# Pooled attention and a top-1 expert layer on one core: partial sums of keys moved up, and the pooled keys of later batches turned by VectorE and a trip through DRAM

## The chip, the core and the metric

The kernel runs on one core of a Trainium2 chip. The metric is the time of one execution on the device in microseconds (us): 2063.51 us is the median of three runs of the kernel before (2062.11 to 2064.42). TensorE (PE in the profile) does matrix products, VectorE (DVE) and ScalarE (ACT) work element by element, GpSimd (POOL) does so too and issues scattered transfers, and SyncE's queue (SP) issues nearly all other DMA transfers.

## The reference, cut to what matters

```python
# q: 4 x 12288 x 128, kv: 4 x 384 x 32 x 128, w_sr: 128 x 128
kv_pool = kv.reshape(B, H // 4, 4, W // 4, 4, C).mean(axis=(2, 4))   # 768 keys for each batch
k = v = kv_pool.reshape(B, -1, C) @ w_sr
a = softmax(q @ k.T / sqrt(C))
x = (a @ v).reshape(B * N, C)                                        # 49152 tokens
# a layer of 8 experts (128 -> 1024 -> 128): each token goes to its best expert
expert = argmax(x @ w_gate); gate = softmax(x @ w_gate)[expert]
out = gate * (relu(x @ w1[expert]) @ w2[expert])
```

## The kernel before

The 49152 tokens are worked off in 96 tiles of 512. For each tile the kernel forms the scores against the batch's 768 keys, the softmax, the weighted values, the choice of expert, and the expert layer with the expert that most tokens of the tile (or of two neighbouring tiles) chose; the tokens left over are worked off at the end. All large products are three products of split numbers (`mm3`, lines 293 to 296): high times high, high times low, low times high. So one product shows as lines L294, L295 and L296.

Everything is written into one plan, `at(t, function)`, and the plan is emitted in order of `t`. A tile is 16 units of plan time. The table `AT` holds the offsets. The plan has no effect on the chip but the order of the instructions on each engine: each engine works its queue in order and waits where an operand is not there. SP's queue is in order too, so a transfer that waits holds up all transfers behind it.

Keys come in six blocks of 128 for each batch (`keys`, L301). A block's raw rows are 16 vectors for each key, 1 MB in four transfers (L317).

- First batch (`b` is 0): loaded at the very start, before anything else can run. Blocks 0 and 2 are summed by VectorE in eight reductions (L335) and turned by one TensorE transpose (L343). Blocks 1, 3, 4 and 5 are summed and turned by TensorE at once, with 16 products against the identity that accumulate (L325). The first q tile is loaded by four transfers (L289) between blocks 2 and 3.
- Later batches: one block every 48 units, which is three tiles, some twenty tiles ahead of use. VectorE sums it in eight reductions spread over the time (`pool` 22.7, step 3.5, so the last stands at 47.2), then `turn` (47.27) puts one 128x128 transpose on TensorE (L343), which writes to a PSUM bank.

After that the two ways are the same: `mean` copies the turned block from PSUM to SBUF on ScalarE with the factor 1/16 (L347), `project` multiplies it twice by `w_sr` on TensorE (L358, L359), and `high_kv` and `low_kv` split the results into `kh`, `vh` (ScalarE) and `kl`, `vl` (VectorE). The turn and the projection each take one PSUM bank from the pool that the expert layer's products use.

The first six tiles turn their probabilities by TensorE; all later ones turn 32x32 squares on VectorE (L473) and finish the turn by writing to DRAM (`pd<-pb`, L480) and reading back in another order (`pt<-pd`, L491 or L495). In the trace the names are those of the tiles: `pooled` is the sum of a block, `pooledT` its turned form, `pt`, `pth`, `pb` probabilities or, early, raw keys and weights, `hh` and `hlow` the expert's hidden values, `wt` its weights.

Of the kernel before, what the change touches and what calls it, by code (L numbers as in the profile page):

```python
# [30 lines left out]


AT = {
    "keys": -0.65, "load": 3.81, "loads": 2.45, "pool": 22.7, "pools": 3.5, "turn_k": 47.27, "turn_q": 2.25,
    "high_q": 4.43, "low_q": 6.71, "maxima": 0.94, "exps": 1.78, ("first_p", 0): 6.14, ("first_p", 1): 3.88,
    ("first_p", 2): 4.75, ("first_p", 3): 4.14, ("first_p", 4): 4.69, ("first_p", 5): 7.37, "first_high": 0.45,
    "first_low": 1.47, "first_values": 2.68, "turn_p": 2.71, ("send_p", 0): 9.0, ("send_p", 1): 16.32, ("fetch_p",
    0): 12.18, ("fetch_p", 1): 22.11, ("high_p", 0): 28.75, ("high_p", 1): 31.23, ("high_p", 2): 31.41, "low_p":
    2.88, ("values", 0): 32.61, ("values", 1): 37.47, ("values", 2): 38.87, ("values", 3): 38.06, ("values", 4):
    40.04, ("values", 5): 41.81, "copy_x": 0.6, "turn_x": 2.61, "logits": 0.46, "gate_exp": 5.86, "gate": 7.55,  # L40
    "ranks": 0.42, "home": 1.04, "places": 4.21, "put_x": 5.65, "high_x": -0.89, "low_x": 3.3, "begin": 83.05,
    "begin_raw": 55.73, "where": -11.29, "raw_cut": -0.42, "raw_cuts": 3.72, "single": 7.95, "spare": -0.19, "ends":
    64.6, "turn_m": -1.68, "high_m": 0.53, "low_m": 3.37, "first": 4.6, "high_h": 0.39, "low_h": 1.61, "second":
    4.8, "copy_y": 0.35, "pads": 3.85, "split": -7.13, "splits": 13.77, "split_cut": 4.58, "split_keep": 8.34,
    "turn_y": 1.84, "move_y": 0.65, "fetch_y": 6.15, "order_y": 13.25, "store_y": 14.0, "rows_y": 4.66, "small":
    -62.58, "square_x": -2.0, "keep_x": 6.88, ("fetch_w", 0): 38.97, ("fetch_w", 1): 47.76, "turn_q_first": -1.28,
    "high_q_first": 5.95, "low_q_first": 11.25, "maxima_first": 0.95, "exps_first": 1.78, "copy_x_first": 0.6,
    "turn_x_first": 2.61, "logits_first": 0.31, "gate_exp_first": 5.2, "gate_first": 9.09, "ranks_first": 0.72,
    "home_first": 0.92, "places_first": 5.56, "put_x_first": 6.88, "high_x_first": 2.66, "low_x_first": 4.03,
    "square_x_first": -2.28, "keep_x_first": 4.32, "turn_q_last": 2.09, "high_q_last": 0.49, "low_q_last": 4.66,  # L50
    "maxima_last": 0.8, "exps_last": 1.78, "turn_p_last": 2.64, ("last", "send_p", 0): 9.0, ("last", "send_p", 1):
    18.25, ("last", "fetch_p", 0): 14.25, ("last", "fetch_p", 1): 20.87, ("last", "high_p", 0): 28.51, ("last",
    "high_p", 1): 31.23, ("last", "high_p", 2): 31.41, "low_p_last": 2.75, ("last", "values", 0): 32.61, ("last",
    "values", 1): 39.93, ("last", "values", 2): 37.08, ("last", "values", 3): 39.31, ("last", "values", 4): 40.04,
    ("last", "values", 5): 41.81, "copy_x_last": 1.6, "turn_x_last": 2.61, "logits_last": 1.96, "gate_exp_last":
    5.86, "gate_last": 7.55, "ranks_last": 0.42, "home_last": 1.03, "places_last": 4.21, "put_x_last": 6.72,
    "high_x_last": -0.83, "low_x_last": 3.3, "square_x_last": -1.7, "keep_x_last": 6.86, ("late", 0): 0.0, ("late",
    1): 0.0, ("late", 2): 16.47, ("half", 0): 67.27, ("half", 1): 74.89, "read": 9.0, ("gather", 0): 18.15,
    ("gather", 1): 15.91, "gathers": 16.0, "count": 62.0, "ask": 74.77, "order_y_first": 11.43, "order_y_last":
    9.25, "store_y_first": 12.26, "store_y_last": 10.0, ("tile", 0): 0.0, ("tile", 1): 0.0, ("tile", 2): -0.02,  # L60
    ("tile", 3): 0.0, ("tile", 4): 0.0, ("tile", 5): 0.02, ("tile", 6): -0.15, ("tile", 7): 0.0, ("tile", 8): 0.0,
    ("moe", 0): 0.2, ("moe", 1): 0.27, ("moe", 2): 0.12, ("moe", 3): 0.69, ("moe", 4): 0.07, ("moe", 5): -0.44,
    ("moe", 6): -3.41, ("moe", 7): 0.0, "where_raw": -8.43, "weights_raw": -5.73, ("weights", 0): -10.38,
    ("weights", 1): -0.95,
}
# [19 lines left out]
def tile_pooled_attention_top1_moe(ctx: ExitStack, tc, q, kv, w_sr, w_gate, w1, w2, out):  # L85
# [215 lines left out]
    def keys(t, b, step):  # L301
        kvv = kv[b].rearrange("(hb i) (wb j) c -> hb wb i (j c)", i=POOL, j=POOL)
        own = {}

# [65 lines left out]
        def high_kv(kb):  # L370
            pr = own["pr", kb]
            src = ordered(pr[:, :P])
            nc.scalar.mul(out=columns(own["kh"], kb), in_=src, mul=scale)
            high(own["vh"][:, kb], pr[:, P : P + C])

        def low_kv(kb):
            pr = own["pr", kb]
            src = ordered(pr[:, :P])
            nc.vector.scalar_tensor_tensor(
                out=columns(own["kl"], kb), in0=src, scalar=scale, in1=columns(own["kh"], kb).bitcast(F32),  # L380
                op0=ALU.mult, op1=ALU.subtract,
            )
# [852 lines left out]
```

## Time and profile before

| what | value |
|---|---|
| median of three runs | 2063.51 us |
| the profiled execution | 2064.57 us, of which the trace's span is 2062.8 us |
| busy share of the span, TensorE / VectorE / GpSimd / ScalarE | 97% / 80% / 73% / 70% |
| chain of work that ended last: TensorE / VectorE / DMA | 81% / 7% / 4% |
| DMA | 484.79 MB, 235 GB/s on average |

Matrix products are pipelined, and their spans in the trace overlap: a 128x512 product shows as 0.39 us, but the next one starts 0.23 to 0.24 us later. So the busy share of TensorE says little; the distance between the starts of two products says what one costs.

### The profile page before, as it was taken

The numbers are of one execution on the slowest core, as the hardware profiler recorded it, in microseconds if no ns is written. First come the engines' busy times: TensorE is split into PE (matmuls) and PEld (weight loads), VectorE is DVE, ScalarE is ACT, GpSimd is POOL, SyncE is SP. The second block draws the span as 40 slices with busy tenths as digits, with TensorE's granted clock in tenths as the row PEclk, the third lists the DMA queues.
The fourth block names the chain that finished last, engine by engine and source line by source line (L and its number), as shares of the span: only waits on it lengthen the run. The fifth ranks groups of instructions, "written<-read, shape, count | busy, mean of one in ns | idle before, by whom it ended". The sixth has DMA issues, their size and how long they took to land.

```text
span 2062.8 us, 32814 instructions
## 1 busy us (share of the span) xinstructions
PE 1994.2 (97%) x9642; PEld 1658.0 (80%) x9642; DVE 1650.5 (80%) x3340; ACT 1442.2 (70%) x2775; POOL 1514.5 (73%) x1589
## 2 busy tenths in 40 slices
PE   6899899999999999999999999999999999999998
PEld 5677678888888888888888888888888888888877
DVE  4678788888888888888788888888877888788755
ACT  3676666777777777777777767677677777767654
POOL 2776677777777777677777777776778777778872
PEclk9999999999999999999999999999999999999999
DMA  9899999898789878877778978787778978777651
GB/s 233 264 270 263 253 229 237 231 237 222 219 260 298 246 229 243 231 244 220 230 228 278 290 225 239 227 256 226 227 218 263 279 215 242 212 217 240 213 195 51
DMA packets 508398, 484.79 MB, mean 235 GB/s; under 512 B 235808, under 2 KB 440481, under 8 KB 506160
## 3 DMA queue, kind: packets, MB, share of 16 engines
q1 hardware_dynamic: 495280, 482.06, 79.3%
q0 software_dynamic: 12928, 0.54, 0.5%
q8 instruction: 78, 1.28, 0.3%
q14 instruction: 112, 0.92, 0.1%
HBM read 330.39 MB, written 234.68 MB: 274 GB/s over the span
## 4 chain that ended last, share of the span: by engine, by line
PE 81%; DVE 7%; issue 4%; DMA 4%; POOL 2%; ACT 1%; SPq 1%; DVEq 0%; POOLq 0%; ACTq 0%
PE ps L294 27%; PE ps L295 26%; PE ps L296 26%; DVE hlow L1047 1%; DVE nmax L450 1%; DMA pt<-pd 1%; DVE pooled L335 1%; PE ps L640 1%; DMA pth<-in_moe_w_dram 1%; DMA qb<-in_q_dram 1%; DVE xq L658 1%; POOL pt L281 1%; DMA pd<-pb 1%; DVE pb L473 1%; DMA ws<-pth 0%
## 5 line engine op out<-in xcount | busy, mean ns | idle before, releaser
L281 POOL TENSOR_TENSOR pt<-pt,pth 128x1024 fp32r<-128x1024 f32 x270 | 646.5, 2410 | 273.7 <-ACT pth L278 253.4
L1043 ACT ACTIVATE hh<-ps 128x512 fp32r<-128x512 f32 x776 | 465.4, 600 | 308.7 <-PE ps L296 294.5
L1047 DVE SCALAR_TENSOR_TENSOR hlow<-ps,hh 128x512 fp32r<-128x512 f32 x776 | 520.4, 671 | 43.8 <-ACT hh L1043 43.2
L458 ACT ACTIVATE prob<-ps,nmax 128x768 f32<-128x768 f32 x384 | 347.6, 905 | 242.5 <-DVE nmax L450 234.3
L450 DVE TENSOR_REDUCE nmax<-ps 128x1 f32<-128x768 f32 x384 | 364.3, 949 | 153.1 <-PE ps L296 152.8
L787 POOL DMA_INDIRECT xs<-row,dst x384 | 381.5, 993 | 119.1 <-issue 90.4
L473 DVE STREAM_TRANSPOSE pb<-prob 128x768 f32<-128x768 f32 x360 | 349.1, 970 | 71.7 <-ACT prob L458 71.6
L294 PE MATMUL ps<-xh,wt 128*128 128x512 f32 x768 | 312.6, 407 | 0.0
L294 PE MATMUL ps<-hh,wt 128*128 128x512 f32 x768 | 305.6, 398 | 0.9 <-DVE yt L1072 0.4
L296 PE MATMUL ps<-xh,wt 128*128 128x512 f32 x768 | 301.6, 393 | 2.1 <-POOL wt L281 2.1
L295 PE MATMUL ps<-hlow,wt 128*128 128x512 f32 x768 | 302.8, 394 | 0.0
L295 PE MATMUL ps<-xl,wt 128*128 128x512 f32 x768 | 302.7, 394 | 0.0
L296 PE MATMUL ps<-hh,wt 128*128 128x512 f32 x768 | 300.5, 391 | 0.0
L294 PE MATMUL ps<-kh,qh 128*128 128x384 f32 x768 | 266.3, 347 | 10.8 <-ACT prob L458 9.4
L278 ACT CAST pth<-pt 128x1024 fp32r<-128x1024 f32 x270 | 276.3, 1062 | 0.0
L296 PE MATMUL ps<-kh,ql 128*128 128x384 f32 x768 | 261.5, 340 | 1.2 <-POOL ql L281 1.2
L295 PE MATMUL ps<-kl,qh 128*128 128x384 f32 x768 | 261.1, 340 | 0.0
L295 PE MATMUL ps<-pt,vh 128*128 128x512 f32 x540 | 213.4, 395 | 2.6 <-POOL pt L281 2.5
L294 PE MATMUL ps<-pth,vh 128*128 128x512 f32 x540 | 212.3, 393 | 0.0
L296 PE MATMUL ps<-pth,vl 128*128 128x512 f32 x540 | 211.2, 391 | 0.0
L294 PEld LDWEIGHTS ps<-xh,wt 128*128 128x128 f32 x768 | 145.6, 190 | 44.9 <-issue 17.7
L294 PEld LDWEIGHTS ps<-kh,qh 128*128 128x128 f32 x768 | 145.7, 190 | 36.8 <-ACT prob L458 18.4
(176 smaller groups left out, 3250.3 us busy)
## 6 DMA issues: line engine op xcount, KB each, us to landing
pd<-pb SPq DMA_DIRECT2D x180, 768.0 KB
pt<-pd SPq DMA_DIRECT2D x144, 768.0 KB
wt<-ws SPq DMA_DIRECT2D x90, 1024.0 KB
pt<-pd SPq DMA_DIRECT2D x144, 192.0 KB
qb<-in_q_dram SPq DMA_DIRECT2D x384, 64.0 KB
xd<-xq SPq DMA_DIRECT2D x96, 256.0 KB
yd<-yt SPq DMA_DIRECT2D x95, 256.0 KB
yr<-yd SPq DMA_DIRECT2D x95, 256.0 KB
```

What stands on the lines that cost most here:

```text
L278: nc.scalar.copy(out=dst, in_=src)
L281: eng.tensor_tensor(out=dst, in0=src, in1=h.bitcast(F32), op=ALU.subtract)
L294: nc.tensor.matmul(out=ps, lhsT=wh, rhs=xh, start=start, stop=False)
L295: nc.tensor.matmul(out=ps, lhsT=wh, rhs=xl, start=False, stop=False)
L296: nc.tensor.matmul(out=ps, lhsT=wl, rhs=xh, start=False, stop=stop)
L335: nc.vector.reduce_sum(out=own["pooled", kb][:, cs], in_=own["raw", kb].rearrange("p r (j c) -> p c r j", c=C)[:, cs], axis=AX.XY,)
L450: nc.vector.tensor_reduce(out=nmax, in_=own["s", g][:, :, :NH], op=ALU.max, axis=AX.XY, negate=True)
L458: nc.scalar.activation(out=prob.rearrange("p (h k) -> p h k", h=2), in_=own["s", g][:, :, :NH], func=AF.Exp, bias=own["nmax", g], scale=1. ...
L473: nc.vector.transpose(out=own["pb"][:, g // HG, :, :, :, g % HG], in_=prob)
L787: put = nc.gpsimd.indirect_dma_start(out=xs, out_offset=bass.IndirectOffsetOnAxis(ap=unit["dst"][:, g : g + 1].bitcast(U32), axis=0), in_= ...
L1043: nc.scalar.activation(out=hh, in_=own["hp", f], func=AF.Relu)
L1047: nc.vector.scalar_tensor_tensor(out=hl, in0=own["hp", f], scalar=0.0, in1=own["hh", f].bitcast(F32), op0=ALU.max, op1=ALU.subtract,)
```

## The change

Keys of the later batches: the eight reductions start a little earlier and stand closer together. The TensorE transpose is gone. In its place `square` turns the 32x32 squares of the block on VectorE, `send` writes the 64 KB to DRAM, and `fetch` reads them back in four transfers that put the squares where they belong. `project` stands 12.43 units behind `square` (it stood 1.5 units behind `turn`). The mean's factor goes into `high_kv` and `low_kv`, so ScalarE's copy from PSUM (`mean`) is gone for these batches.

First batch: block 4 is summed by VectorE and turned by one TensorE transpose, as blocks 0 and 2 are, and the first q tile is loaded behind all six blocks; the second q tile is loaded later too.

A number of other offsets in `AT` change as well; two of them are named here. `gathers` is the distance between the scattered reads for the left-over tokens; with a smaller one they are done earlier. `("weights", 1)` is the fetch of an expert's second matrix. The values' products stand in another order among the others.

```diff
 AT = {
-    ... "pool": 22.7, "pools": 3.5, "turn_k": 47.27, ...
+    ... "pool": 21.6, "pools": 3.34, "turn_k": 47.27, ...
...
-    ("gather", 1): 15.91, "gathers": 16.0, ...
+    ("gather", 1): 15.2, "gathers": 11.62, ...
...
-    ("weights", 1): -0.95,
+    ("weights", 1): 1.08, "square_k": 0.0, "send_k": 0.8, "fetch_k": 7.14, "project": 12.43, ("load_q", 0): -19.2,
+    ("turn_q", 0): -3.1, ("high_q", 0): 0.3, ("low_q", 0): 2.5, ("load_q", 1): -12.0,
 }
...
+        mean_of = 1.0 / (POOL * POOL) if b else 1.0
...
+        def square(kb):
+            assert own["parts", kb] == C // CP
+            own["squares", kb] = kp.tile([P, P], F32, name="pooledT")
+            nc.vector.transpose(out=own["squares", kb], in_=own["pooled", kb])
+
+        def send(kb):
+            own["kd", kb] = dp.tile([P, C], F32, name="kd", bufs=2)
+            nc.sync.dma_start(out=own["kd", kb], in_=own["squares", kb])
+
+        def fetch(kb):
+            own["pT", kb] = kp.tile([P, P], F32, name="pooledT")
+            for n in range(QT):
+                ns = slice(n * SQ, (n + 1) * SQ)
+                nc.sync.dma_start(
+                    out=own["pT", kb][ns].rearrange("r (k c) -> r k c", k=QT),
+                    in_=own["kd", kb][:, ns].rearrange("(k r) c -> r k c", k=QT),
+                )
...
-            nc.scalar.mul(out=columns(own["kh"], kb), in_=src, mul=scale)
-            high(own["vh"][:, kb], pr[:, P : P + C])
+            nc.scalar.mul(out=columns(own["kh"], kb), in_=src, mul=scale * mean_of)
+            nc.scalar.mul(out=own["vh"][:, kb], in_=pr[:, P : P + C], mul=mean_of)
...
-            summed = b or kb in (0, 2)
+            summed = b or kb in (0, 2, 4)
...
-                at(u, turn, kb)
+                if b:
+                    for fn, name in ((square, "square_k"), (send, "send_k"), (fetch, "fetch_k")):
+                        at(u + AT[name], fn, kb)
+                else:
+                    at(u, turn, kb)
...
-            at(u + 0.4, mean, kb)
-            at(u + 1.5, project, kb)
-            at(u + 2.0, high_kv, kb)
-            at(u + 3.2, low_kv, kb)
+            if not b:
+                at(u + 0.4, mean, kb)
+                u += 1.5
+            else:
+                u += AT["project"]
+            at(u, project, kb)
+            at(u + 0.5, high_kv, kb)
+            at(u + 1.7, low_kv, kb)
...
-        at(t - 38, load)
-        u = t + when("turn_q", i) - 16
+        at(AT.get(("load_q", i), t - 38), load)
+        u = t + AT.get(("turn_q", i), when("turn_q", i)) - 16
```

TensorE's queue at the ninth block of the later batches (the third of the third batch), before: the transpose of `pooled` stands between two products of the expert layer, and the projection follows after nine products.

```order
L296 MATMUL ps<-hh,wt_123 128x512
L343 MATMUL ps<-ident,pooled 128x128
L294 MATMUL ps<-xh,wt_123 128x512
L295 MATMUL ps<-xl,wt_123 128x512
L296 MATMUL ps<-xh,wt_123 128x512
L294 MATMUL ps<-kh,qh 128x384
L295 MATMUL ps<-kl,qh 128x384
L296 MATMUL ps<-kh,ql 128x384
L294 MATMUL ps<-kh,qh 128x384
L295 MATMUL ps<-kl,qh 128x384
L296 MATMUL ps<-kh,ql 128x384
L358 MATMUL ps<-pooledT,wsr_sb 128x128
```

The same block in the changed kernel, where the lines of `mm3` are L295 to L297: this is the place of its projection, 77 rows behind the place where the transpose stood.

```order
L295 MATMUL ps<-hh,wt_123 128x512
L296 MATMUL ps<-hlow,wt_123 128x512
L297 MATMUL ps<-hh,wt_123 128x512
L378 MATMUL ps<-pooledT,wsr_sb 128x128
L379 MATMUL ps<-wsr_sb,pooledT 128x128
L295 MATMUL ps<-xh,wt_123 128x512
```

So between VectorE's last sum and the projection there is no instruction of TensorE any more that reads the block.

SP's queue at the eighth block of the later batches, before (`keyrows` are the raw rows of the next block, `yr` and `yd` belong to the output, `xd` keeps x for the left-over tokens):

```order
L480 DMA pd<-pb 128x1536
L1087 DMA yr<-yd 128x4x128
L903 ISA
L903 DMA wt_122<-ws 128x2048
L317 DMA keyrows<-in_kv_dram 128x1x512
L661 DMA xd<-xq 128x512
L317 DMA keyrows<-in_kv_dram 128x1x512
L491 DMA pt<-pd 128x4x384
```

And in the changed kernel:

```order
L354 DMA kd<-pooledT 128x128
L511 DMA pd<-pb 128x1536
L1118 DMA yr<-yd 128x4x128
L319 DMA keyrows<-in_kv_dram 128x1x512
L692 DMA xd<-xq 128x512
L934 ISA
L934 DMA wt_122<-ws 128x2048
L319 DMA keyrows<-in_kv_dram 128x1x512
L360 DMA pooledT<-kd 32x4x32 x4
L522 DMA pt<-pd 128x4x384
```

The block's write stands ahead of the probabilities' second write, and its four reads stand ahead of the probabilities' second read, with two more transfers moved past each other.

SP's queue at the start, before (`pt` and `pb` hold raw keys here; `qb` is a q tile):

```order
L317 DMA pt<-in_kv_dram 128x1x512 x4
L289 DMA qb<-in_q_dram 32x16x32 x4
L317 DMA pb<-in_kv_dram 128x1x512 x4
L317 DMA pt<-in_kv_dram 128x1x512 x4
L317 DMA pb<-in_kv_dram 128x1x512 x4
L289 DMA qb<-in_q_dram 32x16x32 x4
```

And in the changed kernel:

```order
L319 DMA pt<-in_kv_dram 128x1x512 x4
L319 DMA pb<-in_kv_dram 128x1x512 x4
L319 DMA pt<-in_kv_dram 128x1x512 x4
L319 DMA pb<-in_kv_dram 128x1x512 x4
L290 DMA qb<-in_q_dram 32x16x32 x8
```

The four transfers of the first q tile have moved behind those of the last three blocks of keys.

## Rows read from the trace of the kernel before

**Rows 1.** The page, its first line.
```profile
span 2062.8 us, 32814 instructions
```

**Rows 2.** Waits of TensorE: us in total, times, longest; whole span, then 300 to 1940 us.
```profile
PE ps L343 <- DVE pooled L335: 16.4, 18, 2.1
...
PE ps L343 <- DVE pooled L335: 13.3, 16, 1.0
```

**Rows 3.** Timeline of TensorE: start, us, instruction, idle before and releaser; ninth block.
```profile
794.91 0.40 PE L296 MATMUL ps<-hh,wt 128*128 128x512 f32 x1
796.31 0.33 PE L343 MATMUL ps<-ident,pooled 128*128 128x128 f32 x1 [1.00 <-DVE pooled L335]
796.39 0.48 PE L294 MATMUL ps<-xh,wt 128*128 128x512 f32 x1
796.71 0.40 PE L295 MATMUL ps<-xl,wt 128*128 128x512 f32 x1
796.95 0.39 PE L296 MATMUL ps<-xh,wt 128*128 128x512 f32 x1
```

**Rows 4.** Timeline of TensorE, the transpose of the tenth block.
```profile
857.01 0.33 PE L343 MATMUL ps<-ident,pooled 128*128 128x128 f32 x1 [0.64 <-DVE pooled L335]
```

**Rows 5.** Timeline of TensorE, first score products of tiles 32, 38, 73 and 79.
```profile
674.77 0.34 PE L294 MATMUL ps<-kh,qh 128*128 128x384 f32 x1
...
797.18 0.34 PE L294 MATMUL ps<-kh,qh 128*128 128x384 f32 x1
...
1506.58 0.33 PE L294 MATMUL ps<-kh,qh 128*128 128x384 f32 x1
...
1625.53 0.34 PE L294 MATMUL ps<-kh,qh 128*128 128x384 f32 x1
```

**Rows 6.** Stretches: length, busy us of each engine (instructions), clock, DMA share, GB/s.
```profile
15.00:20.00 5.00, 2.81 (x23) 2.41 (x22) 2.56 (x8) 1.31 (x6) 0.00 (x0) 1.00 1.10 208
20.00:25.00 5.00, 4.63 (x38) 4.12 (x36) 2.36 (x6) 0.91 (x5) 0.00 (x0) 1.00 1.06 267
...
180.00:240.00 60.00, 52.47 (x243) 41.94 (x242) 46.17 (x83) 42.47 (x81) 39.86 (x27) 1.00 0.97 250
...
614.00:736.00 122.00, 120.37 (x578) 100.17 (x577) 104.53 (x206) 88.25 (x170) 92.70 (x98) 1.00 0.87 266
```

**Rows 7.** Groups by line and form, VectorE's transposes: busy, mean ns | idle before.
```profile
L473 DVE STREAM_TRANSPOSE pb<-prob 128x768 f32<-128x768 f32 x360 | 349.1, 970 | 71.7 <-ACT prob L458 71.6
...
L428 DVE STREAM_TRANSPOSE qt<-qb 128x512 f32<-128x512 f32 x96 | 67.7, 706 | 3.2 <-POOL ql L281 2.6 <-issue 0.6
```

**Rows 8.** Timeline of SP: the probabilities' second write and the read behind it.
```profile
797.30 0.33 SPq L480 DMA_DIRECT2D pd<-pb  x1
...
801.66 0.37 SPq L491 DMA_DIRECT2D pt<-pd  x1
```

**Rows 9.** Instructions of the q tiles' transfers, 500 to 1500 us: ns min/median/max.
```profile
L289 SPq DMA_DIRECT2D qb<-in_q_dram x196: 338/602/1888, 508.1 to 1482.9; - x196
```

**Rows 10.** Chain of work that ended last, 190 to 230 us: start, us, transfer.
```profile
197.18 9.77 DMA pt<-pd
...
216.14 7.27 DMA pd<-pb
```

**Rows 11.** Timeline of the start, all engines.
```profile
9.81 4.02 SPq L289 DMA_DIRECT2D qb<-in_q_dram  x4
...
25.54 3.84 PE L325 MATMUL ps<-ident,pt 128*128 128x128 f32 x32 [0.60 <-DVE vl L281]
...
30.34 3.74 PE L325 MATMUL ps<-ident,pb 128*128 128x128 f32 x32
...
37.62 0.44 PE L296 MATMUL ps<-kh,ql 128*128 128x384 f32 x1 [0.74 <-POOL ql L281]
```

**Rows 12.** Timeline of GpSimd, then of TensorE, near the end.
```profile
1975.14 1.09 POOL L973 DMA_INDIRECT xb<-xd,idx  x1 [0.38 <-issue]
...
1983.89 0.79 PE L295 MATMUL ps<-pt,vh 128*128 128x512 f32 x1 [2.52 <-POOL pt L281]
```

More of the change, by code (lines that the diff above doesn't have):

```diff
@@ L33 @@
 AT = {
-    "keys": -0.65, "load": 3.81, "loads": 2.45, "pool": 22.7, "pools": 3.5, "turn_k": 47.27, "turn_q": 2.25,
-    "high_q": 4.43, "low_q": 6.71, "maxima": 0.94, "exps": 1.78, ("first_p", 0): 6.14, ("first_p", 1): 3.88,
+    "keys": -0.65, "load": 3.81, "loads": 2.45, "pool": 21.6, "pools": 3.34, "turn_k": 47.27, "turn_q": 2.25,
+    "high_q": 4.43, "low_q": 6.06, "maxima": 0.94, "exps": 1.78, ("first_p", 0): 6.14, ("first_p", 1): 3.88,
     ("first_p", 2): 4.75, ("first_p", 3): 4.14, ("first_p", 4): 4.69, ("first_p", 5): 7.37, "first_high": 0.45,
-    "first_low": 1.47, "first_values": 2.68, "turn_p": 2.71, ("send_p", 0): 9.0, ("send_p", 1): 16.32, ("fetch_p",
+    "first_low": 1.47, "first_values": 2.68, "turn_p": 2.45, ("send_p", 0): 9.0, ("send_p", 1): 16.32, ("fetch_p",
@@ L38 @@
     0): 12.18, ("fetch_p", 1): 22.11, ("high_p", 0): 28.75, ("high_p", 1): 31.23, ("high_p", 2): 31.41, "low_p":
[L39 to L42, printed above, removed]
+    2.88, ("values", 0): 32.61, ("values", 1): 35.3, ("values", 2): 39.86, ("values", 3): 38.06, ("values", 4):
@@ L43 @@
+    40.04, ("values", 5): 41.93, "copy_x": 0.6, "turn_x": 2.61, "logits": 0.64, "gate_exp": 5.86, "gate": 7.55,
+    "ranks": 0.42, "home": 0.63, "places": 4.21, "put_x": 5.4, "high_x": -0.89, "low_x": 3.3, "begin": 83.05,
+    "begin_raw": 55.73, "where": -11.29, "raw_cut": -0.42, "raw_cuts": 3.72, "single": 7.87, "spare": -0.11, "ends":
     64.6, "turn_m": -1.68, "high_m": 0.53, "low_m": 3.37, "first": 4.6, "high_h": 0.39, "low_h": 1.61, "second":
     4.8, "copy_y": 0.35, "pads": 3.85, "split": -7.13, "splits": 13.77, "split_cut": 4.58, "split_keep": 8.34,
-    "turn_y": 1.84, "move_y": 0.65, "fetch_y": 6.15, "order_y": 13.25, "store_y": 14.0, "rows_y": 4.66, "small":
@@ L46 @@
-    -62.58, "square_x": -2.0, "keep_x": 6.88, ("fetch_w", 0): 38.97, ("fetch_w", 1): 47.76, "turn_q_first": -1.28,
-    "high_q_first": 5.95, "low_q_first": 11.25, "maxima_first": 0.95, "exps_first": 1.78, "copy_x_first": 0.6,
+    "turn_y": 2.13, "move_y": 0.65, "fetch_y": 6.15, "order_y": 13.25, "store_y": 14.0, "rows_y": 5.34, "small":
+    -62.58, "square_x": -1.68, "keep_x": 6.88, ("fetch_w", 0): 38.97, ("fetch_w", 1): 47.76, "turn_q_first": -1.28,
+    "high_q_first": 5.95, "low_q_first": 11.25, "maxima_first": 0.95, "exps_first": 1.66, "copy_x_first": 0.6,
@@ L51 @@
     "maxima_last": 0.8, "exps_last": 1.78, "turn_p_last": 2.64, ("last", "send_p", 0): 9.0, ("last", "send_p", 1):
-    18.25, ("last", "fetch_p", 0): 14.25, ("last", "fetch_p", 1): 20.87, ("last", "high_p", 0): 28.51, ("last",
+    17.52, ("last", "fetch_p", 0): 15.2, ("last", "fetch_p", 1): 20.87, ("last", "high_p", 0): 28.51, ("last",
     "high_p", 1): 31.23, ("last", "high_p", 2): 31.41, "low_p_last": 2.75, ("last", "values", 0): 32.61, ("last",
-    "values", 1): 39.93, ("last", "values", 2): 37.08, ("last", "values", 3): 39.31, ("last", "values", 4): 40.04,
+    "values", 1): 40.4, ("last", "values", 2): 39.56, ("last", "values", 3): 39.67, ("last", "values", 4): 40.17,
     ("last", "values", 5): 41.81, "copy_x_last": 1.6, "turn_x_last": 2.61, "logits_last": 1.96, "gate_exp_last":
@@ L379, in low_kv @@
             nc.vector.scalar_tensor_tensor(
-                out=columns(own["kl"], kb), in0=src, scalar=scale, in1=columns(own["kh"], kb).bitcast(F32),
+                out=columns(own["kl"], kb), in0=src, scalar=scale * mean_of, in1=columns(own["kh"], kb).bitcast(F32),
                 op0=ALU.mult, op1=ALU.subtract,
             )
-            low(own["vl"][:, kb], pr[:, P : P + C], own["vh"][:, kb])
+            nc.vector.scalar_tensor_tensor(
+                out=own["vl"][:, kb], in0=pr[:, P : P + C], scalar=mean_of, in1=own["vh"][:, kb].bitcast(F32),
+                op0=ALU.mult, op1=ALU.subtract,
+            )
             give(pr)
@@ L558, in copy_x @@
             drop(BANK_X)
-        at(t - 38, load)
-        u = t + when("turn_q", i) - 16
+        at(AT.get(("load_q", i), t - 38), load)
+        u = t + AT.get(("turn_q", i), when("turn_q", i)) - 16
         at(u, turn_q)
-        at(u + when("high_q", i), high_q)
-        at(u + when("low_q", i), low_q)
+        at(u + AT.get(("high_q", i), when("high_q", i)), high_q)
+        at(u + AT.get(("low_q", i), when("low_q", i)), low_q)
         step = 16 / G
```

4 lines of the change are left out of this document (2 added, 2 removed).

## The prediction

> **What bounds the kernel now.** I read the page first, then the waits of TensorE, then the timeline where they happen, then the stretches. The span is 2062.8 us [rows 1], and the profiled execution took 2064.57 us, so 1.77 us lie around it. The sum below is made against 2064.57; the median of the three runs, 2063.51, stands 1.06 us under it, and I take that off at the end.
>
> In the waits of TensorE the reader is to see that from 300 to 1940 us there is one row: TensorE waits for the sums of the keys and for nothing else, 16 times, 13.3 us in total [rows 2]. There TensorE sets the pace and every other wait is hidden. Each of the 16 is a block of a later batch. The other two blocks come before 300 us; the row of the whole span has 18 waits and 16.4 us, which leaves 3.1 us for those two.
>
> The period says the same. Six tiles with two blocks take 797.18 - 674.77 = 122.41 us, six tiles without one 1625.53 - 1506.58 = 118.95 us [rows 5]. So a block costs 1.73 us of TensorE's time, and a unit of plan time (a sixteenth of a tile) is 19.83 / 16 = 1.24 us. Before 300 us it is not TensorE alone: from 180 to 240 us it is busy 52.47 of 60 us and the DMA share is 0.97 [rows 6], and the chain of waits runs over transfers that land after 7 and 10 us [rows 10].
>
> **The later batches' blocks.** In the ninth block the product ahead of the transpose starts at 794.91 and the transpose at 796.31, 1.40 us later, where the next product normally starts 0.24 us later (796.71 to 796.95) [rows 3]. The wait costs 1.16 us, though the trace shows 1.00 us as idle, because spans overlap; so 0.16 is to be added to each recorded wait. The transpose itself takes 796.39 - 796.31 = 0.08 us, and the product behind it takes 0.32 us to the next start in place of 0.24, another 0.08. In the tenth block the recorded wait is 0.64 us [rows 4]; the blocks alternate. For 16 blocks: 13.3 us recorded [rows 2], 16 x 0.16 = 2.6 us hidden under spans, 16 x 0.16 = 2.6 us for transpose and product behind. That is 18.5 us, 1.16 for each block. The rest of the 1.73, some 0.57, is mostly the projection, which stays.
>
> All of this goes only if nothing waits in its place. Three things are added.
>
> First VectorE's turn of 128x128. A row of 768 columns takes 970 ns and one of 512 takes 706 [rows 7], 1.03 ns for each column, so 128 columns take about 0.31 us, 18 x 0.31 = 5.6 us in all. VectorE is busy 104.53 of 122 us where blocks are made [rows 6], 86%; with two turns more and 2.3 us less time it is 88%. Cover: VectorE's own slack. Bounds 0 to 5.6 us on the path. Sums that move with it cost nothing by themselves, and ScalarE loses a copy for each block, on an engine that has slack; I price these at nothing.
>
> Second the trip. `project` stands 12.43 units behind `square`, 12.43 x 1.24 = 15.4 us. The trip needs: the turn, 0.3 us; the write's issue to landing, for which the probabilities' write is the nearest row, 801.66 - 797.30 = 4.4 us for 768 KB [rows 8]; four read instructions, 0.60 us each in the median of the similar q transfers [rows 9], 2.4 us; the landing of the last, again 4.4 us. Sum 11.5 us, 3.9 us early. From the other side, the landings of the early part are 7.27 and 9.77 us [rows 10] and the longest such instruction 1.89 us: 0.3 + 7.3 + 4 x 1.9 + 9.8 = 25.0 us, 9.6 us late. I take the first, since its rows lie in the part where 16 of the blocks are.
>
> Third, SP's queue. The write stands ahead of `pd<-pb` and waits for VectorE's turn; queued behind it is that write of probabilities, which waits for VectorE itself. The four reads stand ahead of `pt<-pd`, which is issued some 2.4 us later. ScalarE's cast waits for those probabilities; that TensorE's only wait is L343 [rows 2] means there is slack somewhere behind it. I set 1 us in all for the turn, the trip and the queue: a late one here and there, mostly before 300 us.
>
> On the turn, the Trainium skill (VectorE: DVE Perf Modes, Rules for kernel authors) says that a 128x128 transpose belongs on TensorE where PSUM will do as the target, VectorE's being one of 32x32 squares only. The transpose's own 0.08 us agrees with it; by the rule alone the change would be a loss of all the added work. The row shows beside it the 1.16 us that the wait adds, so this case's trace bears the rule out for the transpose alone. On the trip, DMA: Bandwidth & Descriptors (Specifications) puts line rate at 512 bytes and more for a piece; the reads here come in 128-byte pieces. By rows, the q tile's like pieces go with a fall to 208 GB/s from 267, which agrees.
>
> **Early blocks.** The 3.1 us of two blocks lie where transfers set the pace. Bounds 0 to 3.4; I take 1.0.
>
> **The start.** The q tile ahead of block 3 costs the transfers time: 208 in place of 267 GB/s over 5 us is 0.295 MB, 1.1 us, and its own 0.26 MB at 267 GB/s are 1.0 us [rows 6]. So the last block's keys land 2.1 us earlier. TensorE's passes over blocks 4 and 5 follow each other, 25.54 and 30.34 us, and take 3.84 and 3.74 us [rows 11]; with block 4 on VectorE one pass, 3.8 us, leaves the path. The first scores, whose third product starts at 37.62 us, come between 2.1 and 3.8 us earlier; the q tile now lands last and its turn, casts and GpSimd's low part come behind it, so I take 3. How much lasts? From 180 to 240 us the DMA share is 0.97, and the bytes are the same. Bounds 0 and 3.8 us; I take 1.5.
>
> **The end.** TensorE waits 2.52 us for GpSimd at 1983.89 us, and the product after the wait shows 0.79 us against 0.39 [rows 12]. A scattered read of 1.09 us with 0.38 us idle stands ahead of that work on GpSimd, and the reads move earlier. Bounds 0 to 4; I take 1.5.
>
> **Sum.** 18.5 + 1.0 + 1.5 + 1.5 - 1.0 = 21.5 us. 2064.57 - 21.5 - 1.06 = 2042.0 us.
>
> **Rivals.** *The trip comes late* (the slower side). TensorE then waits at the projection, with its whole queue behind it. The point from which it decides: more than 15.4 + 1.16 = 16.6 us for the trip. At 18 us a block waits 2.6 and loses 1.4 net: 16 x 1.4 = 22 us more, less the 4 us of start, early part and end: 2063.5 + 18 = about 2082 us. For it: landings of 7 to 10 us early, and SP waits in order. Against it: 4.4 us in the part that counts. This is also the mechanism by which the skill's rule on transposes (same page) would come out right.
>
> *Half of it comes back as another wait.* VectorE at 88% gives `hlow` or the score maxima late, or the shorter wait merely uncovers the next one: half of 18.5 stays, 9.3, with start and end 2.5: 2063.5 - 11.8 = 2052 us. For it: the wait gave all other engines a rest of 1.2 us for each block. Against it: the stretches without blocks have no wait at all.
>
> *More than the sum.* All of the start, early part and end come in: 18.5 + 3.8 + 3.4 + 4 = 29.7: 2034 us. For it: the product after the long wait near the end takes twice as long as others, so a shorter wait may give back more than itself. Against it: transfers at a share near 1 early.
>
> *The change doesn't do what it says*: the trip is as long as the wait, no gain: 2063 us.
>
> **How the numbers follow.** Forecast 0.72, with its own range 2036 to 2049; half of it back 0.14 (2052); more 0.04 (2034); no gain 0.03; late trip 0.07 (2082). The range reaches from 2034, the sum of upper bounds, to 2056, beyond the half case with 5.6 us of VectorE's turns partly on the path; the late trip and no gain are left out. A measurement here tells some 0.2%, 4 us, from no change. Faster: 0.72 + 0.14 + 0.04 = 0.90; same 0.03; slower 0.07.
>
> **What would show it.** Right: no row of TensorE waiting for `pooled` after 300 us; six tiles with two blocks at about 120.1 us (122.41 less 2 x 1.16); `pooledT` by VectorE at 0.3 us; no wait of TensorE or its weight load at the projection; the third product of the first scores near 34.6 us; a wait under 1.2 us near 1980 us. Wrong: the projection waiting for the DMA, new rows of waits for `hlow` or `nmax` in the stretches with blocks, or a period above 121.3 us there.

## The result, and the profile after

The changed kernel takes 2046.21 us (median of 4 runs, 2045.36 to 2047.12) against 2063.97 us for the kernel before on the same chip: ratio 0.9915, 95% interval [0.9898, 0.9933]. It is faster by 17.8 us, 0.85%; the forecast was 21.5 us. The profiled execution took 2046.93 us, with a span of 2045.2 us against 2062.8 [rows 1].

The waits of TensorE from 300 to 1940 us, where the kernel before had 16 waits for the pooled keys [rows 2]:

```profile
PE ps L296 <- POOL pt L282: 1.5, 2, 1.0
```

The row of the pooled keys is gone and nothing as large stands in its place. In the whole span only two such waits are left, both in the first batch:

```profile
PE ps L345 <- DVE pooled L337: 1.1, 2, 0.6
```

Now the ninth block's way, first VectorE's last sum and its turn with SyncE's transfers, then TensorE at the projection (this answers to [rows 3, 8]):

```profile
784.55 0.57 DVE L337 TENSOR_REDUCE pooled<-keyrows 128x16 f32<-128x256 f32 x1
788.38 0.29 DVE L350 STREAM_TRANSPOSE pooledT<-pooled 128x128 f32<-128x128 f32 x1
788.70 0.33 SPq L354 DMA_DIRECT2D kd<-pooledT  x1
789.08 0.95 SPq L511 DMA_DIRECT2D pd<-pb  x1
792.87 2.18 SPq L360 DMA_DIRECT2D pooledT<-kd  x4
795.13 0.72 SPq L522 DMA_DIRECT2D pt<-pd  x1
...
802.58 0.40 PE L297 MATMUL ps<-hh,wt 128*128 128x512 f32 x1
802.82 0.39 PE L378 MATMUL ps<-pooledT,wsr_sb 128*128 128x128 f32 x2
803.04 0.39 PE L379 MATMUL ps<-wsr_sb,pooledT 128*128 128x128 f32 x2
803.18 0.47 PE L295 MATMUL ps<-xh,wt 128*128 128x512 f32 x1
803.49 0.39 PE L296 MATMUL ps<-xl,wt 128*128 128x512 f32 x1
```

The projection starts 0.24 us after the product ahead of it, the usual step, and has no bracket: no wait. It stands 802.82 - 788.38 = 14.4 us behind the turn; from the fourth block on this room is 14.1 to 14.4 us, in the first three it is 16.0, 12.2 and 15.0. The two products of the projection cost 803.18 - 802.82 = 0.36 us and the product behind them 0.08 more than usual.

The first score products of the tiles that [rows 5] showed:

```profile
667.30 0.33 PE L295 MATMUL ps<-kh,qh 128*128 128x384 f32 x1
...
787.80 0.33 PE L295 MATMUL ps<-kh,qh 128*128 128x384 f32 x1
...
1488.89 0.34 PE L295 MATMUL ps<-kh,qh 128*128 128x384 f32 x1
...
1607.96 0.34 PE L295 MATMUL ps<-kh,qh 128*128 128x384 f32 x1
```

Six tiles with two blocks take 120.50 us in place of 122.41, six without 119.07 in place of 118.95. The stretch with two blocks is 1.91 us shorter, 0.96 for each block; a block still costs (120.50 - 119.07) / 2 = 0.72 us.

A new small wait is part of what is left. `tot` is a sum that VectorE makes for the choice of expert and that a product of TensorE reads. Near 709 us: a partial sum of keys and `tot` on VectorE, the weight load and the product on TensorE:

```profile
708.02 0.60 DVE L337 TENSOR_REDUCE pooled<-keyrows 128x16 f32<-128x256 f32 x1
...
709.78 0.27 DVE L727 TENSOR_REDUCE tot<-oh 128x8 bf16<-128x64 f32 x1
709.85 0.10 PEld L747 LDWEIGHTS <-upper 128*128 128x128 bf16 x1 [0.26 <-issue]
710.10 0.17 PE L747 MATMUL ps<-tot,upper 128*128 128x8 bf16 x1
```

The product ahead starts at 709.62 and this one 0.48 us later, at the end of VectorE's sum; 0.26 more than usual, once in two blocks. It is not in the waits, because spans overlap. In VectorE's queue a partial sum of keys now stands ahead of this `tot`, at 708.02 us; in the kernel before it stood behind, at 717.00 us, with `tot` at 716.80.

The groups by line and form give VectorE's turn (compare [rows 7]), and the table by stretches its share (compare [rows 6]):

```profile
L350 DVE STREAM_TRANSPOSE pooledT<-pooled 128x128 f32<-128x128 f32 x18 | 5.0, 280 | 0.0
```

```profile
614.00:736.00 122.00, 121.91 (x584) 101.73 (x584) 105.28 (x210) 88.64 (x170) 93.71 (x101) 1.00 0.88 268
```

At the start the third product of the first scores (compare [rows 11]), and near the end the product that had waited 2.52 us for GpSimd [rows 12]:

```profile
31.89 0.45 PE L297 MATMUL ps<-kh,ql 128*128 128x384 f32 x1
...
1966.08 0.50 PE L296 MATMUL ps<-pt,vh 128*128 128x512 f32 x1 [0.19 <-POOL pt L282]
```

The first product after this wait took 0.79 us before [rows 12]. The stretches behind the wait, before and after, in the form of [rows 6], show why: TensorE's granted clock was 0.50 (1.2 GHz) before and is 1.00 (2.4 GHz) after.

```profile
1983.90:1987.30 3.40, 3.40 (x8) 2.73 (x9) 0.24 (x1) 0.60 (x1) 3.40 (x2) 0.50 0.99 405
...
1966.00:1969.40 3.40, 3.32 (x14) 2.74 (x15) 1.38 (x2) 2.26 (x4) 3.40 (x3) 1.00 0.89 286
```

**Where the 17.6 us of the span come from.** Take the start of each tile's first score product in both traces; the difference is the lead. At tile 13 (289 us before) it is 3.0 us, at tile 76 (1566 us), behind the last block, 17.6, at tile 93 (1904 us) 16.5, at TensorE's last product 19.4, and at the end of the span 17.6. So: start and early blocks 3.0, the 16 blocks 14.6, the tiles behind -1.1, the last part of TensorE +2.9, and behind its last product -1.8.

### The profile page after: what moved, and what is told of

Read it like the earlier page. It is cut to its first block, busy times and chain, and to the rows that moved or that the text cites. A ratio compares the mean times of both kernels' runs of the same rounds, so it can differ in the third digit from the quotient of the medians.

```text
span 2045.2 us, 32918 instructions
## 1 busy us (share of the span) xinstructions
PE 1986.2 (97%) x9593; PEld 1652.2 (81%) x9593; DVE 1655.0 (81%) x3366; ACT 1438.1 (70%) x2757; POOL 1515.4 (74%) x1589
## 4 chain that ended last, share of the span: by engine, by line
PE 81%; DVE 4%; POOL 1%; DMA 1%; issue 1%; ACT 0%; SPq 0%; DVEq 0%; ACTq 0%
PE ps L295 27%; PE ps L296 26%; PE ps L297 26%; DVE hlow L1078 1%; PE ps L671 1%; DVE nmax L481 0%; DVE pooled L337 0%; DVE pb L504 0%; POOL pt L282 0%; DMA pd<-pb 0%; DMA keyrows<-in_kv_dram 0%; DVE xq L689 0%; DMA pt<-pd 0%; POOL xb L1004 0%; PE ps L379 0%
## 5 line engine op out<-in xcount | busy, mean ns | idle before, releaser
L818 POOL DMA_INDIRECT xs<-row,dst x384 | 381.9, 995 | 120.5 <-issue 91.0
L295 PE MATMUL ps<-xh,wt 128*128 128x512 f32 x768 | 311.9, 406 | 0.5 <-DVE pb L282 0.5
L295 PE MATMUL ps<-hh,wt 128*128 128x512 f32 x768 | 303.6, 395 | 0.9 <-DVE yt L1103 0.4
L297 PE MATMUL ps<-xh,wt 128*128 128x512 f32 x768 | 301.3, 392 | 0.9 <-POOL wt L282 0.9
L297 PE MATMUL ps<-hh,wt 128*128 128x512 f32 x768 | 300.4, 391 | 0.0
L295 PE MATMUL ps<-kh,qh 128*128 128x384 f32 x768 | 267.4, 348 | 10.8 <-ACT prob L489 10.5
L297 PE MATMUL ps<-kh,ql 128*128 128x384 f32 x768 | 261.7, 341 | 0.6 <-POOL ql L282 0.5
L297 PE MATMUL ps<-pth,vl 128*128 128x512 f32 x540 | 211.5, 392 | 0.0
L295 PE MATMUL ps<-pth,vh 128*128 128x512 f32 x540 | 211.4, 391 | 0.0
L295 PEld LDWEIGHTS ps<-xh,wt 128*128 128x128 f32 x768 | 144.6, 188 | 47.0 <-issue 14.7
L295 PEld LDWEIGHTS ps<-kh,qh 128*128 128x128 f32 x768 | 145.3, 189 | 38.6 <-ACT prob L489 22.1
```

The costliest lines, as they stand in the source:

```text
L295: nc.tensor.matmul(out=ps, lhsT=wh, rhs=xh, start=start, stop=False)
L297: nc.tensor.matmul(out=ps, lhsT=wl, rhs=xh, start=False, stop=stop)
L818: put = nc.gpsimd.indirect_dma_start(out=xs, out_offset=bass.IndirectOffsetOnAxis(ap=unit["dst"][:, g : g + 1].bitcast(U32), axis=0), in_= ...
```

## The experiments

A tile's first score product serves again as the mark. "Blocks" is what a kernel's trace gains on the trace of before between tile 13 and tile 76; the kernel before ran in each of the three groups (2064.30, 2063.65 and 2063.58 us).

| run | median us | ratio, 95% interval | lead at tile 13 | blocks |
|---|---|---|---|---|
| e1 start alone | 2064.59 | 1.0004 [0.9994, 1.0013] | 2.9 | -3.5 |
| e2 sums earlier alone | 2050.42 | 0.9933 [0.9919, 0.9946] | 5.4 | 10.8 |
| e13 trip alone | 2051.81 | 0.9946 [0.9931, 0.9960] | 4.4 | 11.0 |
| e9 sums, trip, gathers | 2048.13 | 0.9928 [0.9915, 0.9942] | 1.0 | 14.1 |
| e3 change, TensorE turns | 2049.73 | 0.9928 [0.9914, 0.9941] | 1.5 | 11.1 |
| e5 change, late sums | 2048.03 | 0.9919 [0.9906, 0.9932] | 1.2 | 12.4 |
| e4 change, old start | 2049.04 | 0.9932 [0.9919, 0.9945] | 3.1 | 14.1 |
| e8 change, old gathers | 2047.50 | 0.9919 [0.9906, 0.9932] | 2.5 | 13.6 |
| e11 change, turn thrice | 2051.86 | 0.9940 [0.9927, 0.9953] | 2.8 | 9.7 |
| e12 projection 2.4 us sooner | 2049.48 | 0.9932 [0.9916, 0.9948] | 2.4 | 13.0 |
| e6 projection 4.9 us sooner | 2092.07 | 1.0139 [1.0119, 1.0159] | -8.4 | -16.8 |
| e10 the change again | 2047.85 | 0.9925 [0.9912, 0.9938] | 2.0 | 14.7 |

**Earlier sums alone (e2).**

```diff
 # before
-"pool": 22.7, "pools": 3.5
+"pool": 21.6, "pools": 3.34
```

> The kernel before with one edit: the later batches' sums are placed 1.1 units of plan time earlier and 0.16 closer to each other, so that the last of the eight stands 2.2 units, some 2.7 us, earlier; TensorE still turns the pooled keys. Theory A (the time was TensorE's wait for the sums, whoever turns them): the recorded wait of 0.6 to 1.0 us a block is gone after 300 us, the 0.16 us of the turn and of the product behind it stay, so about 0.9 of the 1.16 us a block go: 16 x 0.9 = 14 us, 2050 us (2047 to 2053). Theory B (VectorE works a backlog in order, so an earlier place brings the sums no earlier; only taking the turn off TensorE's queue removes the wait): the row of the wait stays at 13 us, 2062 to 2065 us.

2050.42 us: theory A. TensorE still turns the keys and no longer waits for them; its row of waits after 300 us is another:

```profile
PE ps L716 <- DVE tot L696: 2.0, 8, 0.3
```

The sums alone bring 13.9 us; the whole change brought 17.8 us in its first measurement and 15.7 us beside e10. VectorE was late by about a microsecond at one reader, and an earlier place mends that.

**The trip alone (e13).**

```diff
 # before, with square, send and fetch of the change
+"square_k": 0.0, "send_k": 0.8, "fetch_k": 7.14, "project": 12.43,
-at(u, turn, kb)
+for fn, name in ((square, "square_k"), (send, "send_k"), (fetch, "fetch_k")):
+    at(u + AT[name], fn, kb)
```

> The kernel before with only the trip: VectorE's turn and DRAM in the later batches, projection as in the change; the sums, the first batch and all other places as before. Theory A' (either the earlier sums or taking the turn off TensorE's queue removes the wait, and the trip has room even behind late sums): 2064 - 16 x 0.95 = about 2049 us (2047 to 2052), no row of the wait for the sums and none at the projection after 300 us. Rival (the sums late by about 1 us make the trip late): a row of TensorE waiting for the transfers at the projection, 2056 us or more.

2051.81 us at the upper edge of theory A': the wait for the sums is gone this way as well, and none stands at the projection. The wait for `tot` is twice that of e2:

```profile
PE ps L747 <- DVE tot L727: 4.0, 8, 1.0
```

So either half removes the wait, and they don't add: 10.8 and 11.0 us alone in the blocks, 14.1 to 14.7 together.

**The change without the trip (e3).**

```diff
-for fn, name in ((square, "square_k"), (send, "send_k"), (fetch, "fetch_k")): ...
+at(u, turn, kb)
+at(u + 0.4, mean, kb)
```

> The changed kernel with TensorE's transpose and ScalarE's mean back in place of VectorE's squares and the trip through DRAM, in the later batches; the earlier sums, the start and all other places stay as changed. Theory A: no wait for the sums, only 16 x 0.16 = 2.6 us for the transposes come back: 2046.2 + 2.6 = about 2049 us (2047 to 2051). Theory B: the wait for the sums is back, 10 us or more: 2057 to 2062 us.

2049.73 us, as theory A has it. In the blocks it gives 11.1, 3.5 us less than the change; that is what the trip adds once the sums are early, a little more than the 2.6 us of TensorE's transposes. The Trainium skill (VectorE: DVE Perf Modes, Rules for kernel authors) puts this transpose on TensorE; with the wait gone by other means this case's runs still favour VectorE's turn with its trip, by these 3.5 us in the trace, though the intervals of the times overlap.

The wait for `tot` stands here too, though VectorE turns no keys in these batches: the product ahead and the product of `tot`, again 0.48 us apart, in the same eight places as in the changed kernel.

```profile
711.99 0.39 PE L297 MATMUL ps<-pth,vl 128*128 128x512 f32 x1
712.47 0.17 PE L740 MATMUL ps<-tot,upper 128*128 128x8 bf16 x1
```

So this wait does not come from VectorE's turn.

**The change with late sums (e5).**

```diff
-"pool": 21.6, "pools": 3.34
+"pool": 22.7, "pools": 3.5
```

> The changed kernel with one edit: the sums are placed as late as in the kernel before (the last of eight 2.2 units, some 2.7 us, later); VectorE still turns them and they still go through DRAM. Theory A with the trip as forecast (11.5 us of the 15.4 us between the turn and the projection): the later sums hold up VectorE's turn by 1 to 2 us, the projection still waits for nothing: 2046 us (2045 to 2048). Rival (the trip needs 14 us and more, so the earlier sums were there for the trip): the projection waits 1 us or more at each of 16 blocks: 2060 us or more.

2048.03 us, at the edge of theory A: no wait at the projection. The wait for `tot` comes back in seven places:

```profile
PE ps L747 <- DVE tot L727: 2.6, 7, 0.9
```

**The start alone (e1).**

```diff
 # before
-summed = b or kb in (0, 2)
+summed = b or kb in (0, 2, 4)
+("load_q", 0): -19.2, ("turn_q", 0): -3.1, ("high_q", 0): 0.3, ("low_q", 0): 2.5, ("load_q", 1): -12.0,
```

> The kernel before with only the first batch changed: its fifth block summed by VectorE, the first two q tiles loaded later. Theory A (the 3 us by which the changed kernel leads at 300 us are the start's and they last): 2064.0 - 3.3 = 2060.7 us, the first scores some 5 us earlier. Rival (transfers set the pace up to 300 us at a share near 1 and the bytes are the same, so the lead is given back): 2063 to 2065 us, with the first scores as early.

2064.59 us: nothing. The first scores come 5.2 us earlier and 2.9 us are left at tile 13, but the waits for the sums from 300 to 1940 us grow to

```profile
PE ps L344 <- DVE pooled L336: 14.7, 16, 1.7
```

One of them, at 672.54 us, shows it: 1.67 us in place of 1.00. The rival has the time right and the reason wrong: the lead is not lost up to 300 us but later, and in two places alone. From tile 3 up to 668 us it stays at 2.7 to 3.2 us. From there to 674 us and from 1154 to 1160 us (times of the kernel before), in the first blocks of the third and the fourth batch, it falls by 1.7 and 1.9 us: TensorE waits 0.2 to 0.4 us for ScalarE's `prob`, 0.3 us for VectorE's `yt` and 1.7 us in place of 1.0 for the sums. In the other blocks waits and lead change by less than 0.2 us, so there VectorE's sums come earlier by the same lead. Why these two blocks differ was not found.

**The change without its start (e4).**

```diff
-summed = b or kb in (0, 2, 4)
+summed = b or kb in (0, 2)
 # and the loads and turns of the first two q tiles as before
```

> The changed kernel with the first batch's part undone: the fifth block is summed by TensorE's passes again and the first two q tiles are loaded and turned as before. Alone on the kernel before, this part gained 2.9 us by 300 us and gave it back in longer waits for the sums (14.7 us recorded in place of 13.3). Theory C (a head start is worth nothing before the first waits of TensorE alone, but with those waits gone it lasts): without it 2046.2 + 3 = about 2049 us (2047.5 to 2050.5). Rival (the lead is eaten by the stretch up to 300 us, where transfers and VectorE set the pace): 2045 to 2047 us.

2049.04 us, between 1.2 us above e10 and 2.8 above the first measurement, with overlapping intervals; the profiled execution, at 2046.03, was the fastest of its five. Not decided: the start is worth 0 to 3 us here.

**Before's other places with sums, trip and gathers (e9).**

```diff
 # before, with square, send and fetch
-"pool": 22.7, "pools": 3.5 ... ("gather", 1): 15.91, "gathers": 16.0
+"pool": 21.6, "pools": 3.34 ... ("gather", 1): 15.2, "gathers": 11.62
```

> The kernel before with three parts of the change and no others: the earlier sums, the later batches' turn by VectorE and DRAM, and the gathers of the last part earlier; first batch and all other places as before. If the parts add: 2050.4 (earlier sums alone) - 3 for the transposes and the wait for tot that came with them - 1 to 2.5 for the wait near the end = about 2045.5 us (2044 to 2047). Rival (the other moved places were needed for the trip, without them VectorE and the transfers' queue give the sums' gain back): 2049 us or more.

2048.13 us, between the two theories, and not told apart from the change by its interval. 14.1 us in the blocks: the many other numbers of the change hardly matter there, though TensorE's waits show `tot` with 2.1 us in 8 places, as in e2, where the changed kernel has its 0.26 us without a row.

**The gathers as before (e8).**

```diff
-("gather", 1): 15.2, "gathers": 11.62 ... ("weights", 1): 1.08
+("gather", 1): 15.91, "gathers": 16.0 ... ("weights", 1): -0.95
```

> The changed kernel with the gathers and the last weights placed as in the kernel before. Theory D (the wait for GpSimd near 1980 us, 2.5 us before and 0.2 after, went by these places): the wait of 2 us or more is back there and the end of TensorE's work is some 2.5 us later; of this 1 to 2.5 us show in the time: 2047.2 to 2048.7 us. Rival (that wait went by the earlier end of the tiles ahead of it, whatever the gathers do, or the last store's landing takes it all): 2045.5 to 2047 us.

The wait is back, theory D in the trace:

```profile
1967.96 0.80 PE L296 MATMUL ps<-pt,vh 128*128 128x512 f32 x1 [2.54 <-POOL pt L282]
```

In the 3.4 us behind the wait the granted clock is 0.51. TensorE gains 0.5 us from tile 93 to its end in place of 2.9, and loses 0.4 us from tile 76 to tile 93 in place of 1.1: in sum 0.1 us against 1.8 (1.7 in e10). So at TensorE the edit, the gathers with this fetch of weights, is worth some 1.7 us. But the time, 2047.50 us, is that of the unaltered change (2047.85), so its effect on the time lies below what these runs can tell.

**The projection sooner (e6, e12).**

```diff
-"project": 12.43
+"project": 8.5      # e6
+"project": 10.5     # e12
```

> The changed kernel with the projection 3.93 units of plan time, some 4.9 us, sooner behind VectorE's turn, so that the trip has about 10.5 us. Theory E (trip of 11.5 us as forecast): the projection waits some 1 us in each of 16 blocks for the transfers and loses about that: 2046 + 10 to 20 = 2056 to 2066 us. Rival (the trip is much shorter than forecast, or the wait is hidden): no wait, 2046 to 2048 us. Second rival (the trip really takes 14 us and more, with hardly any room left in the changed kernel): 2080 us or more.

2092.07 us: slower than before, and beyond theory E's range. The second rival has a time like it, but its trip of 14 us and more is found in the first block alone. The waits from 300 us, and two ahead of it, are as large as 5.3 us:

```profile
PE ps L378 <- DMA pooledT<-kd: 23.0, 13, 2.9
```

```profile
PE ps L378 <- DMA pooledT<-kd: 7.9, 2, 5.3
```

Where the reads are late, the trace shows how long the trip is. A block in the later part, and the first of all, on VectorE, SyncE and TensorE:

```profile
811.59 0.29 DVE L350 STREAM_TRANSPOSE pooledT<-pooled 128x128 f32<-128x128 f32 x1
811.91 0.33 SPq L354 DMA_DIRECT2D kd<-pooledT  x1
812.28 0.69 SPq L511 DMA_DIRECT2D pd<-pb  x1
813.07 0.38 SPq L1118 DMA_DIRECT2D yr<-yd  x1
813.50 1.03 SPq L319 DMA_DIRECT2D keyrows<-in_kv_dram  x1
814.58 0.60 SPq L692 DMA_DIRECT2D xd<-xq  x1
815.22 0.55 SPq L319 DMA_DIRECT2D keyrows<-in_kv_dram  x1
815.81 2.21 SPq L360 DMA_DIRECT2D pooledT<-kd  x4
822.12 0.46 PE L378 MATMUL ps<-pooledT,wsr_sb 128*128 128x128 f32 x2 [1.81 <-DMA pooledT<-kd]
```

```profile
189.14 0.27 DVE L350 STREAM_TRANSPOSE pooledT<-pooled 128x128 f32<-128x128 f32 x1
189.43 0.34 SPq L354 DMA_DIRECT2D kd<-pooledT  x1
194.97 2.52 SPq L360 DMA_DIRECT2D pooledT<-kd  x4
204.57 0.77 PE L378 MATMUL ps<-pooledT,wsr_sb 128*128 128x128 f32 x2 [5.27 <-DMA pooledT<-kd]
```

In the later part 822.1 - 811.6 = 10.5 us: 0.3 for the turn, 3.9 from the write's issue to the first read's, 2.2 for the four reads' issue, 4.1 from there to the projection. In the 3.9 us SyncE issues five other transfers with hardly a pause, so in this block the reads stand behind these and not behind the landing of the write, which no row shows. In the 13 blocks that waited after 300 us the trip took 9.9 to 11.2 us; early it is 15.4 us in the first block and 9.8 in the second. In the changed kernel itself the first block has 203.17 - 187.20 = 16.0 us, so it clears by some 0.6 us if its trip is as long as in e6:

```profile
187.20 0.27 DVE L350 STREAM_TRANSPOSE pooledT<-pooled 128x128 f32<-128x128 f32 x1
...
203.17 0.46 PE L378 MATMUL ps<-pooledT,wsr_sb 128*128 128x128 f32 x2
```

These waits cost more than themselves. Behind three of them TensorE's granted clock falls to half, at 393.5, 823.6 and 1253.7 us; between 300 us and tile 76 the changed kernel has 1.00 throughout. The second of the three, behind a wait of 1.81 us:

```profile
823.60:827.00 3.40, 3.40 (x11) 3.12 (x10) 0.67 (x3) 1.75 (x5) 2.92 (x3) 0.50 0.23 60
```

> The changed kernel with the projection 1.93 units, 2.4 us, sooner: 13.0 us for the trip. With 10.5 us the recorded waits were 23 us in 13 blocks after 300 us, 1.8 us each, so the trip there ends some 12.3 us behind the turn's place. Theory E as measured (a fixed trip of about 12.3 us): no wait in the later part, and hardly one before 300 us: 2046 to 2051 us. Rival (the trip's length scatters, and any loss of room costs): the waits for the transfers are there in several blocks, 2055 us or more.

2049.48 us, as theory E has it: no wait at the projection after 300 us, one of 1.2 us in the first block. The smaller step costs less than 2 us, the larger one 44 (both against the 2047.85 of e10): the trip has an edge, and behind it nearly every block pays.

**VectorE's turn three times (e11).**

```diff
-nc.vector.transpose(out=own["squares", kb], in_=own["pooled", kb])
+for n in range(3):
+    nc.vector.transpose(out=own["squares", kb], in_=own["pooled", kb])
```

> The changed kernel with VectorE's turn of the pooled keys done three times in place of once (the same result written again): 2 x 0.3 us more of VectorE for each of 18 blocks, 11 us in all. Theory G (VectorE's slack hides its turn): 2046 to 2049 us, as the changed kernel, and no new wait. Rival (part of the forecast's other half: VectorE's turn delays what TensorE reads from VectorE): 5 us or more on top, 2052 to 2058 us, with rows of TensorE waiting for tot, hlow or pb.

2051.86 us, 4.0 above e10 in the same group: neither nothing nor the whole. The groups of VectorE and the waits of TensorE from 300 us:

```profile
L351 DVE STREAM_TRANSPOSE pooledT<-pooled 128x128 f32<-128x128 f32 x54 | 16.3, 301 | 1.2
```

```profile
PE ps L748 <- DVE tot L728: 3.1, 7, 0.4
```

In the 16 blocks, 32 turns of 0.30 us, 9.6 us of VectorE, take 14.65 - 9.7 = 5.0 us from the gain, 4.3 of them at `tot`. The half is not a half of each block. `tot` in the seventh block, on VectorE and TensorE, in the changed kernel and then TensorE's product here:

```profile
669.30 0.28 DVE L727 TENSOR_REDUCE tot<-oh 128x8 bf16<-128x64 f32 x1
669.72 0.18 PE L747 MATMUL ps<-tot,upper 128*128 128x8 bf16 x1
...
671.77 0.17 PE L748 MATMUL ps<-tot,upper 128*128 128x8 bf16 x1 [0.44 <-DVE tot L728]
```

With one turn `tot` is ready at 669.58 us, 0.14 us before its product starts, at the usual step of 0.23 us behind the product ahead. With three turns it is ready at 671.72 us, the product starts 0.05 us behind it, and the step is 0.83 us. So some 0.09 us were to spare, and nearly all of the added turns comes out. That is so in seven blocks, every second one; in the blocks between, the step is 0.48 us with one turn and with three. So the turn itself is covered, with hardly anything to spare in every second block.

**The change again (e10).** The changed kernel, with no edit:

> The changed kernel, unaltered, once more, beside the others. Across the profiled runs so far the lead over the kernel before at 310 us lies between 2.1 and 6.7 us with no order in it by edit, and the kernel before itself spreads from 2060.1 to 2068.3 us. Theory F (the stretch up to 310 us, where transfers set the pace, differs by some 3 us from one execution to the next; what lies behind 310 us repeats within 1 us): the lead at 310 us differs from the 3.7 us of the first profile by 1 us or more, the gain from 310 us to the last of the blocks is again 14 us; 2045 to 2049 us. Rival (each program has its own early stretch): 3.7 us again, within 0.5 us.

2047.85 us. The lead at tile 0 is 3.5 us in place of 5.1, at 310 us 2.6 in place of 3.7, just the 1 us that theory F asks for; the blocks give 14.7 us, the 14.6 of the first profile once more. e4, whose later batches are those of the change, gives 14.1 us. So the blocks' gain of a single trace can be compared within some 0.6 us, the lead at tile 13 not within 1 us.

## Why the prediction was right, and where it was off

**The wait is the time: right.** The row goes, and e2, e3, e5 and e13 take the two ways of removing it apart. The forecast priced the whole on taking the turn off TensorE's queue; the runs show that the earlier sums alone do it, so what I priced at nothing ("sums that move with it") was a cure of its own, worth 13.9 us. e13 shows that the cure I forecast would have done too. The change holds both, and either removes the wait.

**The 16 blocks, 18.5 us: mechanism right, size off.** 14.6 and 14.7 in two traces. Counted from the start of one product of TensorE to the next, between tile 13 and tile 76, the waits, 15.9 us with what spans hide, and the transposes are gone as forecast, and 3.9 us come in elsewhere that the forecast did not have, beyond its 1 us for turn, trip and queue.

2.0 us of them are the eight steps to the product of `tot`. The term that failed is again the sums that move with it, "cost nothing by themselves": moved up, one of them stands ahead of `tot`. e2 and e3 have the wait as well, though VectorE turns no keys of the later batches there, 3.3 and 2.0 us counted from the starts; that the sum ahead of `tot` makes it is argued from the order of VectorE's queue. This is a part of the rival "half comes back": the next reader of VectorE is uncovered. VectorE's own turn is covered, as forecast, but with 0.09 us to spare in the block shown under e11, where I had taken a busy share of 88% for slack enough.

1.4 us lie in the scores' products of high times high: 504 of them take 91.2 us from start to start in place of 89.8, in e10 too, where e2 has 89.9. Why was not found. The last 0.5 us are spread over the other products. The period of 120.5 in place of 120.1 us says the same.

**The trip: right in its sum, one part by luck.** Forecast 11.5 us, measured 10.5 in the ninth block. I had 4.4 us for the landing of the write; found are 3.9, but in that block they are the issue of five other transfers, which the sum did not have. Room forecast 15.4, found 14.4; why it is 1 us less was not found. The upper bound of 25.0 was too far; early it is 15.4.

**The late trip as a rival: priced too low.** With the projection 4.9 us sooner it happened. The 16 blocks lose 14.65 + 16.8 = 31.5 us to the change. 23.0 are the recorded waits, 13 x 0.16 = 2.1 are hidden under spans, as the forecast has it for the waits of before, and three stretches of 3.4 us at half the clock cost up to 3 x 1.7 = 5.1 us, an estimate: 30.2 in all. The forecast's price had the waits and not the clock that falls behind them. Some 11 us more go ahead of tile 13, where 7.9 us of waits are recorded.

**Start and early blocks, 2.5 us: right in sum, for reasons not separated.** 3.0 and 2.0 at tile 13. The third product of the first scores came at 31.89 us, 5.7 earlier where I had said about 3, and at the next tile only 1.2 are left. A part of that is the clock: from 36 to 47 us 0.84 of it is granted before and 0.69 after. e1 shows that on the kernel before the lead lasts to 668 us and is lost in two blocks; e4, without the new start, has 3.1 us at tile 13 too and leaves 0 to 3 us for the start in the changed kernel.

**The end, 1.5 us: right at TensorE, not in the time.** The wait fell to 0.19 us and e8 brings it back. From tile 76 TensorE's end gains 1.8 us in sum (-1.1 and +2.9). The product of twice the usual length behind the wait, which the forecast had named as a reason for more, was the clock at half, and it went with the wait. But behind TensorE's last product the span goes on for 7.1 us before and 9.0 after (8.9 in e10), which takes it back. The trace of e4, the change with the old start, has 7.2 there; in the nine traces with the new start it is 7.8 to 9.0 us, in the five without 7.1 to 7.6. So in these traces it goes with the start and not with the gathers; by what way was not found.

## What to carry to other kernels

When an engine with an in-order queue is the bound and waits for one late producer, first try placing the producer's work earlier: two numbers gave as much alone as a new path through DRAM gave alone (10.8 and 11.0 us in the blocks). Removing a wait gives less than the wait by what the producer's next reader then waits, and work that moves up in the producer's queue may delay that reader: look at what it now stands ahead of. A busy share of 86% does not tell how much room is left there; here it was 0.09 us at one reader. A trip through DRAM has an edge: measure its length where it is late, since no wait shows how near the edge it is, and look at what else stands in the queue between its write and its reads.

## What was not expected of the hardware

The kernel before, unaltered, spread from 2058.67 to 2068.25 us in these three groups, 0.5%, so that edits worth 1 to 3 us could be seen in stretches of the traces but not in the times. A part of the spread goes with TensorE's clock: of its 38 executions the ten fastest had a mean granted clock of 0.993 to 0.996, the ten slowest 0.991 to 0.993. The clock also made some waits of TensorE dearer than they look: it fell to half behind the wait of 2.52 us near the end of the kernel before, and behind three of the 13 waits in e6, of 1.8 to 2.9 us, while others as long as 2.1 us left it at 1.00. The same trip through DRAM took 15.4 us where the DMA share was 1.00 (180 to 210 us of e6) and 10.5 us where it was 0.84 (810 to 825 us).
